# Sparse-window attention and a two-layer tail: q, k and x turned by crossbar DMA in batches 1 to 3, scores on half-height arrays, and GpSimd's ring for the early tiles and the weights

## The chip, the cores and the metric

The kernel runs on one core of one Trainium2 chip. The metric is device time in microseconds (us) of one execution. The core's engines are TensorE (PE: matmuls and their weight loads, PEld), VectorE (DVE), ScalarE (ACT), GpSimd (POOL) and SyncE (SP, which here only issues DMAs). Each works through its own instructions in order. Data moves by sixteen DMA engines, which SP's, ACT's and POOL's rings share.

## The reference

Four batches, eight heads, 768 positions, head size 64. A retrieval head attends to everything before it; the other heads only to the first 4 positions (the sink) and to a window of 64. The outcome of the eight heads is a row of 512 for each of 3,072 tokens, and passes through two matrices with h - tanh(h) between them.

```python
scores = q @ k.T / 8                       # (4, 8, 768, 768)
keep   = causal & (retrieval_head | key < 4 | (pos_q - pos_k < 64))
a      = softmax(where(keep, scores, -1e9))
x      = (a @ v).transpose(0, 2, 1, 3).reshape(3072, 512)
h      = x @ w_in                          # (512, 2048)
out    = (h - tanh(h)) @ w_out             # (2048, 512)
```

Which heads are retrieval heads comes as data (`is_retrieval`: three of the eight in this input).

## The kernel before

Work is cut into 12 tiles of 256 tokens, three to a batch: tile t belongs to batch t // 3, and g = t % 3 is its place in the sequence, so that attention grows with g. Within a tile the heads go in four pairs (hp); a unit n is one pair of one tile. Matmuls are in fp16.

For one unit, in order:

- `load` brings q, k and v in fp32 on SP's ring, in packets of 256 bytes (one row of one head). `cast_qk` and `cast_v` turn them to fp16; `t16` holds q and k, `v1` holds v with a column of ones, `vf` a copy of v that is zero for the heads that don't attend far.
- `st_T` turns q and k on PE (four 128x128 transposes into `tp`), then one copy takes q to `qT` and two copies take the two heads' k into `kz`. In `kz` the other head's 64 rows are zero, so that a score matmul contracts over all 128 rows.
- `st_S` (L854) multiplies k blocks by q into `sc`, ACT takes exp into `pt` (L869), DVE multiplies by a mask.
- `st_A` (L920) multiplies `pt` by v into `av`; DVE takes the reciprocal of the sum and scales (L940, L950, L964).
- `st_X`, or `st_X_tile` for ranked tiles, turns x on PE into `xp` and a copy takes it to `xT`.

For one tile, eight `H_unit`s follow (L1033: x by w_in into `ph`; ACT tanh, L1046; DVE h - tanh(h) into `gt`, L1053) and the O groups (L1092: `gt` by w_out into `po`; ACT copies to `ot`, L1068; SP stores it).

From tile 3 on a tile is *ranked*: `by_rank` has sorted the heads by their flags on the chip, and `cast_ranked` (L609, POOL) fetches each head's q, k and v at an offset read from a register, so that pairs 0 and 2 hold all retrieval heads and pairs 1 and 3 are *near* pairs, which need only the block of the query, the block before it and the sink. `st_S_near` (L798) computes near pairs. For them `kz` keeps, behind each 128 keys, a copy of the batch's first 64 keys (`repeat`, L754, POOL), so that 64 late keys of the block before and the sink's block lie side by side. If more than four heads were retrieval heads, the program would be run again in a general form; with this input it isn't.

The order of all engines is not written by hand. Each step is put down with an engine, an estimated duration and what it reads and writes (`op`), and `Plan.run` lays the steps out on the engines by those estimates and by priority; the instructions come out in that order. Which step is put down when is set by slots: slot t * 8 + u holds H unit u of tile t and the O groups of the tile before, and attention of later tiles is spread over the slots. PSUM is divided by tags: `sc` two buffers of two banks, `h` two, `m` and `o` one each.

Of the kernel before, what the change touches and what calls it, by code (L numbers as in the profile page):

```python
# [16 lines left out]
class Plan:  # L17
# [16 lines left out]
    def op(self, eng, ns, fn, r=(), w=(), dma=None, prio=None, port=False):  # L34
# [14 lines left out]
        for key in (*r, *w):  # L49
            if isinstance(key, tuple) and key[0] in self.bufs:  # L50
                tag, at = key[:2]
                deps.update(self.users.get((tag, at - self.bufs[tag]), ()))
                self.users.setdefault((tag, at), []).append(i)
# [5 lines left out]
    def run(self):  # L59
        n = len(self.ops)  # L60
        users = [[] for _ in range(n)]
# [8 lines left out]
        rings = {"SP": [], "POOL": []}  # L70
# [31 lines left out]
        while len(order) < n:  # L102
# [34 lines left out]
            if dma:  # L137
                packets, each = dma
                rings["POOL" if e == "POOL" else "SP"].append(
                    [i, t + ns + 300, each, packets * each / 16]  # L140
                )
            else:
                finish(i, t + ns + self.RESULT[e])
# [6 lines left out]
def kernel(  # L150
# [29 lines left out]
    assert n_sink_i <= 128 and window_i <= 128  # L180

    def pool(name, bufs=1, **kw):
        return ctx.enter_context(tc.tile_pool(name=name, bufs=bufs, **kw))

    const = pool("const")
    RAW, T16, PT, XB, GB, XTB, THB, OB = 6, 2, 3, 3, 3, 3, 3, 3
    bufs = dict(
        raw=RAW, t16q=T16, t16k=T16, pt=PT, x16=XB, x16t=2, rinv=XB, gt=GB, xT=XTB, th=THB, ot=OB,
        v1=2, vf=2, sc=2, m=1, h=2, o=1, **{f"qT{hp}": 2 for hp in range(HP)},
    )  # L190
    raw_pool = pool("raw", RAW)
    t16_pool = pool("t16", T16)
    qt_pool = pool("qt", 2)
    v_pool = pool("vp", 2)
    pt_pool = pool("pt", PT)
    x_pool = pool("x", XB)
    xn_pool = pool("xn", 2)
    sm_pool = pool("sm", XB)
    xt_pool = pool("xt", XTB)
    w_pool = pool("w")  # L200
    g_pool = pool("g", GB)
    th_pool = pool("th", THB)
    o_pool = pool("o", OB)
# [3 lines left out]
    HH = H // 2  # L207

    Engine = mybir.EngineType
# [12 lines left out]

    fast = n_sink_i <= 64 and window_i <= 64
    NGEN = H // 2

    KS = [192 if fast and hp % 2 else 128 for hp in range(HP)]
    kz = [
        [const.tile([128, 2, 2 * NG * KS[hp]], FP16, name=f"kz{s}_{hp}") for hp in range(HP)]
        for s in range(2)
    ]  # L230
# [13 lines left out]
    w_in_t = []  # L244
    w_out_t = []

    def program(first):
# [5 lines left out]
        def bank(shape, dt, tag, name):  # L253

            i = rot[tag] = rot.get(tag, -1) + 1
            box = []

            def get():
                if not box:
                    box.append(ps.tile(shape, dt, tag=tag, bufs=bufs[tag], name=name))  # L260
                return box[0]

            return get, (tag, i)

        def lazy(pl, shape, dt, tag, name):
            box = []

            def get():
                if not box:
                    box.append(pl.tile(shape, dt, tag=tag, name=name))  # L270
                return box[0]

            return get


        raws = {}

        def load(t, names="qkv", halves=(None,)):

            b, g = divmod(t, NG)  # L280
            for half in halves:
                h0, nh = (0, H) if half is None else (half * HH, HH)
                for nm in names:
                    src = {"q": q, "k": k, "v": v}[nm]
                    if (nm, t) not in raws:
                        idx = rot["raw"] = rot.get("raw", -1) + 1
                        raws[nm, t] = (
                            lazy(raw_pool, [128, NB, H, D], FP32, "raw", f"raw_{nm}{t}"), idx
                        )
                    r, idx = raws[nm, t]  # L290
                    for i in range(NB):
                        s0 = g * TT + i * 128
                        op(
                            "SP", max(420, 128 * nh * 1.1),
                            lambda r=r, i=i, src=src, s0=s0, h0=h0, nh=nh: nc.sync.dma_start(  # L295
                                out=r()[:, i, h0 : h0 + nh, :],
                                in_=src[b, h0 : h0 + nh, s0 : s0 + 128, :].rearrange("h p d -> p h d"),
                            ),
                            w=[("raw", idx, i, x) for x in (range(2) if half is None else (half,))],
                            dma=(128 * nh, 21.0),  # L300
                        )

        def load_w_in(j, w_after):
            w = lazy(w_pool, [128, HP, 512], FP16, f"win{j}", f"win{j}")
            op(
                "POOL", 900,
                lambda: nc.gpsimd.dma_start(
                    out=w()[:],
                    in_=moe_w_in[:, j * 512 : (j + 1) * 512].rearrange("(cb p) f -> p cb f", p=128),
                ),  # L310
                r=w_after, w=[("win", j)], dma=(512, 80.0),
            )
            w_in_t.append(w)

        def load_w_out(j, w_after):
            w = lazy(w_pool, [128, 4, DM], FP16, f"wout{j}", f"wout{j}")
            op(
                "POOL", 900,
                lambda: nc.gpsimd.dma_start(
                    out=w()[:],  # L320
                    in_=moe_w_out[j * 512 : (j + 1) * 512, :].rearrange("(fb p) m -> p fb m", p=128),
                ),
                r=w_after, w=[("wout", j)], dma=(512, 80.0),
            )
            w_out_t.append(w)


        def zero_kz(eng, s, hp, c0, c1, after=()):
            op(
                eng, (c1 - c0) * 1.06 * KS[hp] / 128 + 20,  # L330
                lambda: engs[eng].memset(
                    kz[s][hp][:].bitcast(FP32)[
                        :, :, c0 * KS[hp] // 256 : c1 * KS[hp] // 256
                    ], 0.0,
                ),
                r=after, w=[("kz", s, hp, g) for g in range(c0 // TT, c1 // TT)],
            )

        if first:
            op(  # L340
                "SP", 400,
                lambda: nc.sync.dma_start(
                    out=retr_i[:], in_=is_retrieval.bitcast(I32).partition_broadcast(128)
                ),
                w=["retr"], dma=(128, 20.0),
            )
        for half in range(2):
            load(0, "qk", (half,))
            load(0, "v", (half,))
        if first:  # L350

            op("POOL", 204, lambda: nc.gpsimd.memset(ones[:], 1.0), w=["ones"])
# [5 lines left out]

# [21 lines left out]

# [16 lines left out]
            if fast:  # L397
                select(mS[0:64, 3, :], ones[0:64, :], 0.0, window_i - 65, -1, 1, "mS3")
                select(mS[64:128, 3, :], ones[64:128, :], 0.0, n_sink_i - 1, 0, -1, "mS3")

            for hp in range(HP):
                zero_kz("DVE", 0, hp, 0, TT)
            for hp in range(HP):
                zero_kz("DVE", 0, hp, TT, S)

# [19 lines left out]
            for h in range(H):  # L425
                op(
                    "DVE", 260,
# [6 lines left out]

            def make_rflag0():

                nc.vector.scalar_tensor_tensor(
                    out=rflag0[:], in0=sinks[:, 0:1].to_broadcast([128, H]), scalar=0.75,
                    in1=rflag[:], op0=ALU.is_ge, op1=ALU.max,
                )  # L440

            op("DVE", 165, make_rflag0, r=["sinks", "rflag"], w=["rflag0"])


        RANK = [4 * (hp % 2) + 2 * (hp // 2) + hh for hp in range(HP) for hh in range(2)]
        regs = {}

        def ranked(t):
            return first and fast and t >= NG

        def by_rank():

            def dve(ns, fn, r, w):
                op("DVE", ns, fn, r=r, w=w)
# [76 lines left out]
            for h in range(NGEN):  # L531
                op(
                    "DVE", 260,
# [7 lines left out]
                "DVE", 200,  # L541
# [7 lines left out]
                "DVE", 150,  # L549
# [14 lines left out]
        t16s = {}  # L564

        def cast_op(e, ns, dst, src, r, w):
            cost = {"ACT": 163 + 0.85 * ns, "DVE": 85 + 0.65 * ns, "POOL": 90 + 0.96 * ns}[e]
            if e == "ACT":
                op(e, cost, lambda: nc.scalar.copy(out=dst(), in_=src()), r=r, w=w)  # L569
            else:  # L570
                op(e, cost, lambda: engs[e].tensor_copy(out=dst(), in_=src()), r=r, w=w, port=True)

        def cast_qk(t, engines, halves=range(2)):

            for half in halves:
                for nm, es in zip("qk", engines):
                    if (nm, t) not in t16s:
                        t16s[nm, t] = lazy(
                            t16_pool, [128, NB, H, D], FP16, f"t16{nm}", f"t16_{nm}{t}"
                        )  # L580
                    c = t16s[nm, t]
                    r, slot = raws[nm, t]
# [693 lines left out]
```

## Time and profile before

| | |
|---|---|
| median of 3 runs | 264.74 us (264.37 to 265.63) |
| span of the profiled execution | 262.6 us |
| its time beside the span | 2.1 us (median less span) |
| PE busy | 239.3 us, 91% |
| VectorE, ScalarE, GpSimd busy | 182.7, 145.0, 99.2 us |
| moved by DMA | 29.88 MB; 75,744 of 83,081 packets under 512 bytes |
| granted TensorE clock | 0.992 |

The span runs from the first to the last instruction; the rest of a run's time lies around it. PE's busy time counts matmuls from their issue to their modelled end, and neighbours overlap, so a busy PE need not be a PE at its peak. The page's other parts give the chain of waits that ended last, the groups of instructions by line and shape, and the DMA queues.

### The profile page before, as it was taken

The numbers are of one execution on the slowest core, as the hardware profiler recorded it, in microseconds if no ns is written. First come the engines' busy times: TensorE is split into PE (matmuls) and PEld (weight loads), VectorE is DVE, ScalarE is ACT, GpSimd is POOL, SyncE is SP. The second block draws the span as 40 slices with busy tenths as digits, with TensorE's granted clock in tenths as the row PEclk, the third lists the DMA queues.
The fourth block names the chain that finished last, engine by engine and source line by source line (L and its number), as shares of the span: only waits on it lengthen the run. The fifth ranks groups of instructions, "written<-read, shape, count | busy, mean of one in ns | idle before, by whom it ended". The sixth has DMA issues, their size and how long they took to land.

```text
span 262.6 us, 6565 instructions
## 1 busy us (share of the span) xinstructions
PE 239.3 (91%) x2420; PEld 177.8 (68%) x2420; DVE 182.7 (70%) x501; ACT 145.0 (55%) x215; POOL 99.2 (38%) x294
## 2 busy tenths in 40 slices
PE   0358998999999899999999999999999999999990
PEld 0146876776777677777777877777777777776660
DVE  7886975666799876678997766587897765654300
ACT  4368666765566465664566655645556747534320
POOL 5165502696994994239972300510700000000000
PEclk9999999999999999999999999999999999999996
DMA  6999999999999294457432811011001011101121
GB/s 138 222 206 194 208 197 201 207 209 241 227 215 226 76 236 99 122 129 185 88 92 57 178 40 42 2 40 41 11 35 40 2 40 42 40 4 41 40 89 46
DMA packets 83081, 29.88 MB, mean 114 GB/s; under 512 B 75744, under 2 KB 80096, under 8 KB 83040
## 3 DMA queue, kind: packets, MB, share of 16 engines
q1 hardware_dynamic: 78672, 25.05, 43.7%
q0 software_dynamic: 4224, 4.19, 9.5%
q8 instruction: 21, 0.34, 0.6%
q14 instruction: 20, 0.16, 0.2%
q10 hardware_dynamic: 144, 0.13, 0.2%
HBM read 27.27 MB, written 6.29 MB: 128 GB/s over the span
## 4 chain that ended last, share of the span: by engine, by line
PE 76%; DMA 8%; SPq 6%; DVE 5%; issue 1%; ACT 0%; POOL 0%; POOLq 0%; DVEq 0%
PE po L1092 30%; PE ph L1033 27%; DMA raw_k<-in_k_dram 8%; PE sc L854 7%; SPq L295 6%; PE av L920 5%; PE tp L716 3%; PE sc L798 2%; PE xp L982 2%; DVE pt L829 1%; DVE gt L1053 1%; DVE kz L704 1%; DVE x16t L950 1%; DVE qT L704 0%; ACT ot L1068 0%
## 5 line engine op out<-in xcount | busy, mean ns | idle before, releaser
L1033 PE MATMUL ph<-xT,win 128*128 128x256 f16 x768 | 101.3, 273 | 0.8 <-DVE gt L1053 0.7
L1092 PE MATMUL po<-wout,gt 128*128 128x512 f16 (+1 forms) x400 | 100.2, 371 | 0.3
L1046 ACT ACTIVATE th<-ph 128x512 f32<-128x512 f32 x96 | 57.4, 598 | 62.9 <-PE ph L1033 61.2
L1053 DVE SCALAR_TENSOR_TENSOR gt<-th,ph 128x512 f16<-128x512 f32 x96 | 65.6, 684 | 29.6 <-ACT th L1046 28.7
L1033 PEld LDWEIGHTS <-win 128*128 128x128 f16 x768 | 72.0, 98 | 16.5 <-DVE gt L1053 1.0
L869 ACT ACTIVATE pt<-sc 128x768 f16<-128x768 f32 (+1 forms) x60 | 53.3, 917 | 21.3 <-PE sc L854 20.7
L1092 PEld LDWEIGHTS <-gt 128*128 128x128 f16 x400 | 35.7, 98 | 20.2 <-issue 0.5
L609 POOL CAST t_q<-raw_q 128x128 f16 x72 | 21.2, 303 | 45.0 <-PE tp L716 44.6
L854 PE MATMUL sc<-qT,kz 128*128 128x256 f16 (+1 forms) x280 | 34.0, 255 | 4.6 <-DVE kz L704 3.3
L920 PEld LDWEIGHTS <-pt 128*128 128x128 f16 x552 | 26.4, 99 | 10.1 <-DVE pt L884 2.2
L854 PEld LDWEIGHTS <-kz 128*128 128x128 f16 x280 | 22.9, 100 | 12.1 <-DVE kz L704 5.6
L704 DVE COPY kz<-tp 64x256 f16<-64x256 f16 x96 | 27.2, 283 | 1.9 <-ACT qT L702 0.4
L920 PE MATMUL av<-v,pt 128*128 128x65 f16 x304 | 27.0, 197 | 1.2 <-DVE pt L884 1.2
L609 POOL CAST t_k<-raw_k 128x128 f16 x72 | 21.9, 313 | 0.1
L812 ACT ACTIVATE pt<-sc 128x1024 f16<-128x1024 f32 (+1 forms) x18 | 17.1, 950 | 8.6 <-PE sc L798 8.5
L950 DVE TENSOR_TENSOR x16t<-av,rinv 128x128 f32 x72 | 20.7, 288 | 1.5
L920 PE MATMUL av<-vf,pt 128*128 128x65 f16 x248 | 20.6, 193 | 1.1 <-DVE pt L829 0.7
L1068 ACT ACTIVATE ot<-po 128x512 f32<-128x512 f32 (+1 forms) x24 | 14.1, 589 | 10.0 <-PE po L1092 9.8
L609 POOL CAST v<-raw_v 128x128 f16 x72 | 18.8, 303 | 1.1 <-DMA raw_v<-in_v_dram 0.9
L716 PE MATMUL tp<-ident,t_q 128*128 128x128 f16 x96 | 14.0, 230 | 5.8 <-ACT t_q L569 5.3
L940 DVE RECIPROCAL rinv<-av 128x4 f32<-128x4 f32 x48 | 8.6, 180 | 15.1 <-PE av L920 14.6
L716 PEld LDWEIGHTS <-t_q 128*128 128x128 f16 x96 | 8.9, 103 | 9.6 <-ACT t_q L569 5.3
(76 smaller groups left out, 191.1 us busy)
## 6 DMA issues: line engine op xcount, KB each, us to landing
out_dram<-ot SPq DMA_DIRECT2D x23, 256.0 KB, 2.2
raw_q<-in_q_dram SPq DMA_DIRECT2D x20, 256.0 KB, 4.2
raw_k<-in_k_dram SPq DMA_DIRECT2D x20, 256.0 KB, 4.7
raw_v<-in_v_dram SPq DMA_DIRECT2D x20, 256.0 KB, 5.0
win<-in_moe_w_in_dram POOLq DMA_DIRECT2D x4, 512.0 KB, 10.6
wout<-in_moe_w_out_dram POOLq DMA_DIRECT2D x4, 512.0 KB, 12.9
raw_q<-in_q_dram SPq DMA_DIRECT2D x8, 128.0 KB, 3.4
raw_k<-in_k_dram SPq DMA_DIRECT2D x8, 128.0 KB, 3.5
```

What stands on the lines that cost most here:

```text
L609: nc.gpsimd.tensor_copy(out=o, in_=r()[:, :, at, :])
L704: nc.vector.tensor_copy(out=dst, in_=src)
L716: nc.tensor.transpose(out=tp()[:, x, i, :], in_=c()[:, i, 2 * hp : 2 * hp + 2, :], identity=ident16[:],)
L812: lambda: nc.scalar.activation(out=pt()[:, :, 0:wid], in_=sc()[:, :, 0:wid], func=AF.Exp, scale=inv_sqrt_d),
L854: nc.tensor.matmul(out=sc()[:, hh, o : o + nb * 128], lhsT=kk[:, hh, jb * KS[hp] : jb * KS[hp] + 128], rhs=qT[n]()[:, q0 * 128 : (q0 + nb) ...
L869: lambda: nc.scalar.activation(out=pt()[:, :, 512 * gi : 512 * gi + wid], in_=sc()[:, :, 0:wid], func=AF.Exp, scale=inv_sqrt_d,),
L920: nc.tensor.matmul(out=av()[:, i, hh, :], lhsT=pt()[:, hh, co : co + 128], rhs=vv, start=(jb == first_jb), stop=(jb == qb),)
L950: nc.vector.tensor_mul(out=x16s[t]()[:, :, at, :], in0=av()[:, :, hh : hh + 1, 0:D], in1=rinv()[:, :, hh : hh + 1].unsqueeze(3).to_broadca ...
L1033: nc.tensor.matmul(out=ph()[:, j, :], lhsT=w_in_t[fb // 4]()[:, cb, f0 : f0 + 128], rhs=xTs[t]()[:, cb, :], start=(cb == 0), stop=(cb == H ...
L1046: lambda: nc.scalar.activation(out=th()[:], in_=ph()[:], func=AF.Tanh, scale=1.0 / XS),
L1053: lambda: nc.vector.scalar_tensor_tensor(out=gts[t]()[:, u * FU : (u + 1) * FU, :], in0=th()[:], scalar=-XS, in1=ph()[:], op0=ALU.mult, op ...
L1092: nc.tensor.matmul(out=po()[:, c0:c1], lhsT=gts[t]()[:, f, ts * 128 : ts * 128 + 128], rhs=w_out_t[f // 4]()[:, f % 4, c0:c1], start=(f == ...
```

## The change

It rewrites much of the kernel around the same tiles, masks and second half.

- **Batch 0, tile 0.** q and k come in packets of 512 bytes (two neighbouring rows), on SP. ACT casts q, DVE casts k; PE turns them; DVE copies both into one buffer `QK` per batch, [128, 8, 768], in which each pair has one row block for q and one for k. `qT` and `kz`, its zeros and their memsets are gone. The flags of the heads come after the first half's turns, the ranking after tile 0's attention.
- **Tiles 1 and 2 and the weights.** All come on POOL's ring, the tiles already cast by the DMA (`load_cast`), in the order tile 1, w_in 0, tile 2, w_in 1 to 3, w_out 0 to 3. Two DVE copies per tile put q and k in order for PE's turn.
- **Tiles 3 to 11.** `load_raw` loads on SP, for tile 3 after w_out 2 has landed and for later ones after w_out 3. `gather` (POOL) takes q and k of a head in one copy, and SP then turns them by two crossbar transposes of [128, 1024] into `QK`. `st_X_tile` is one crossbar transpose on SP into `xT`, whose layout is now [128, block, pair, 128].
- **Scores.** Both heads of a pair are multiplied from their own 64 rows of `QK`, one after the other, into two PSUM banks. `st_S` takes one or two such units at a visit, generic and near ones mixed.
- **Near pairs.** The sink's 64 keys and the 64 late keys of each block lie ready in a buffer `kc`, [128, 2, 4, 128], filled by POOL.
- **Order.** The H units of tiles 0 and 1 alternate by w_in block; O groups follow H by two tiles instead of one; attention of tile t is spread over new stretches of slots (`cut`). The planner sees buffers across the whole program and gets a ring for ACT.

The diff at its core:

```diff
-            for i in range(NB):                      # load: 256-byte packets, SP
-                ...
+    def load_cast(t, after=()):
+            for x, src in enumerate((q, k)):
+                dma("POOL", 1300, lambda x=x, src=src: nc.gpsimd.dma_start(
+                        out=pk()[:].rearrange("p (x h e) -> p x h e", x=2, h=H)[:, x, :, :],
+                        in_=src[b, :, g * TT : (g + 1) * TT, :].rearrange("h (p i) d -> p h (i d)", i=2)),
+                    128 * H, 30.0, r=after, w=[("t16p", ip, x)])
+            ...
+    def load_raw(t, after=()):
+            for i in range(NB):
+                for x, src in enumerate((q, k, v)):
+                    dma("SP", 520, ..., 128 * H, 18.0, r=after, ...)
+    def gather(t):
+            for s_ in range(H):
+                def qk(s_=s_):
+                    at = bass.ds(regs["POOL"][RANK[s_]], 1)
+                    nc.gpsimd.tensor_copy(out=c5()[:, :, :, s_ : s_ + 1, :], in_=r5()[:, :, :, at, :])
+                op("POOL", 400, qk, ...)
+            for i in range(NB):
+                dma("SP", 520, lambda i=i: nc.sync.dma_start_transpose(
+                        out=QKs[b]()[:, :, g * TT + i * 128 : g * TT + i * 128 + 128],
+                        in_=c()[:, i * 2 * H * D : (i + 1) * 2 * H * D]),
+                    1024, 22.0, ...)
+            ...
-    def st_S_near(n): ...
-    def st_S(n, gi): ...
+    def st_S(units):
+            todo, reads, keys, ns = [], [], [], 160
+            ...
+            def mm():
+                for n, gi, b, g, hp, near, sc, key, pieces, wid in todo:
+                    QK = QKs[b]()
+                    for jb, q0, nb, o, comp in pieces:
+                        for hh in range(2):
+                            p_ = slice(64 * hh, 64 * hh + 64)
+                            lhsT = QK[p_, HP + hp, :][:, jb * 128 : jb * 128 + 128]
+                            if comp:
+                                lhsT = kcs[b]()[p_, hp // 2, jb - 1, :]
+                            nc.tensor.matmul(out=sc()[:, hh, o : o + nb * 128], lhsT=lhsT,
+                                rhs=QK[p_, hp, q_0 : q_0 + nb * 128], start=True, stop=True)
-    def st_X_tile(t, half): ...                       # four PE transposes and a copy, twice
+    def st_X_tile(t):
+            dma("SP", 520, lambda: nc.sync.dma_start_transpose(
+                    out=xT()[:].rearrange("p i a c -> p (i a) c"),
+                    in_=xt()[:].rearrange("p i h d -> p (i h d)")), 1024, 22.0, ...)
...
-        LAG = 1
+        slots = [(t, 2 * j + u, None) for j in range(4) for t in range(2) for u in range(2)
+        ] + [(t, u, (t - 2, 4 * u)) for t in range(2, NTT) for u in range(NFU)]
+            cut = (-10.5, -6.0, 2.25, 13.5)
+            lo, hi = base + cut[g], base + cut[g + 1]
+            if ranked(t):
+                gate = [("wout", 2 if b == 1 and g == 0 else 3)]
+                spread_over([lambda t=t, gate=gate: load_raw(t, gate)], lo - 15, lo - 14)
+                spread_over([lambda t=t: gather(t), lambda t=t: spread(t)], lo - 7, lo - 5)
+                spread_over(attention(t), lo, hi)
```

More of the change, by code (lines that the diff above doesn't have):

```diff
@@ L269, in get @@
                 if not box:
-                    box.append(pl.tile(shape, dt, tag=tag, name=name))
+                    shp, dt = shape[tag]
+                    box.append(pools[tag].tile(shp, dt, tag=tag, name=f"{tag}{i}"))
                 return box[0]
-            return get
-        raws = {}
-        def load(t, names="qkv", halves=(None,)):
-            b, g = divmod(t, NG)
[L281 to L290, printed above, removed]
-                    for i in range(NB):
[L292 to L301, printed above, removed]
@@ L328, in zero_kz @@
[L328 to L346, printed above, removed]
@@ L347, in program, with dma, ranked @@
[L347 to L350, printed above, removed]
+            return get, i
+        def dma(ring, ns, fn, packets, each, r=(), w=()):
+            op(ring, ns, fn, r=r, w=w, dma=(packets, each))
+        RANK = [4 * (hp % 2) + 2 * (hp // 2) + hh for hp in range(HP) for hh in range(2)]
+        regs = {}
+        def ranked(t):
+            return first and fast and t >= NG
+        QKs, v1s, vfs, kcs, t16s, raws = {}, {}, {}, {}, {}, {}
@@ new lines, in cast_first, with fn @@
+        def cast_first(half, engines):
+            rq, iq, rv, iv = raws[0]
+            c, ic = t16s[0]
+            n = HH * 128
+            for x in range(2):
+                e = engines[x]
+                cost = {"ACT": 163 + 0.85 * n, "DVE": 85 + 0.65 * n, "POOL": 90 + 0.96 * n}[e]
+                def fn(x=x, e=e):
+                    h0 = half * HH
+                    i_ = rq()[:].rearrange("p (x h i d) -> p x i h d", x=2, h=H, i=2)[
+                        :, x, :, h0 : h0 + HH, :
+                    ]
+                    o_ = c()[:].rearrange("p (x i h d) -> p x i h d", x=2, h=H, i=2)[
+                        :, x, :, h0 : h0 + HH, :
+                    ]
+                    copy(e, o_, i_)
+                op(
+                    e, cost, fn, r=[("rawqk", iq, x, half)], w=[("t16", ic, x, half)],
+                    port=e == "DVE",
+                )
@@ L561, in by_rank @@
                 op(e, 900, get, r=["perm"], w=["regs" + e])
[L564 to L582, printed above, removed]
-                    hs = slice(half * HH, half * HH + HH)
-                    cast_op(
-                        es[half], NB * HH * D, lambda c=c, hs=hs: c()[:, :, hs, :],
-                        lambda r=r, hs=hs: r()[:, :, hs, :],
-                        r=[("raw", slot, i, half) for i in range(NB)], w=[("t16" + nm, t, half)],
-                    )
@@ L703, in copy, with st_T @@
             else:
-                nc.vector.tensor_copy(out=dst, in_=src)
-        def st_T(n, eq="DVE", ek=("DVE", "DVE")):
+                engs[e].tensor_copy(out=dst, in_=src)
+        COPY = {"ACT": 373, "DVE": 288}
+        def st_T(n, engines=("DVE", "DVE")):
             t, hp = divmod(n, HP)
             b, g = divmod(t, NG)
-            tp, key = bank([128, 2, 8, 128], FP16, "sc", f"tp{n}")
-            keys = [(*key, x) for x in range(2)]
-            cq, ck = t16s["q", t], t16s["k", t]
+            half = hp * 2 // HP
+            tp, key = bank([128, 2, NB, 128], FP16, "h", f"tp{n}")
+            keys = [key, key]
+            c, ic = t16s[t]
@@ new lines, in program @@
+        if first:
+            dma(
+                "ACT", 400,
+                lambda: nc.scalar.dma_start(
+                    out=retr_i[:], in_=is_retrieval.bitcast(I32).partition_broadcast(128)
+                ),
+                128, 20.0, w=["retr"],
+            )
+            load_first()
+            constants()
+            iq = raws[0][1]
+            for half in range(2):
+                cast_first(half, ("ACT", "DVE"))
+                for n in (2 * half, 2 * half + 1):
+                    st_T(n, TE)
+                if half == 0:
+                    flags()
+            for half in range(2):
+                for n in (2 * half, 2 * half + 1):
+                    st_S([(n, 0)])
+                if half == 0:
+                    gate = [("rawqk", iq, 0, 0)]
+                    load_cast(1, gate)
+                    for i in range(NB):
+                        cast_v_first(i)
+                    for item in ORDER:
+                        if item == "t2":
+                            load_cast(2, gate)
+                        else:
+                            load_w(*divmod(item, 4), gate)
+        else:
+            for t in range(3):
+                load_cast(t)
+            for n in range(HP):
+                st_T(n, TE)
+                st_S([(n, 0)])
@@ L1168, in program @@
+        for n in range(HP):
             st_A(n, 0)
@@ L1170, in program @@
             st_X(n, "o", "ACT")
-        for half in range(2):
-            cast_qk(1, (("ACT", "ACT"), ("ACT", "ACT")), (half,))
-            cast_v(1, ("POOL", "POOL"), (half,))
-        if first:
-            for j in range(4):
-                load_w_in(j, [("v1", 0, 1, j // 2)])
-        load(2)
-        scale_v(0, "DVE")
-        scale_v(1)
-        if first:
-            for j in range(4):
-                load_w_out(j, [("win", 3)])
-            for hp in range(HP):
-                zero_kz("POOL", 1, hp, 0, S, [("wout", 3)])
-            if fast:
-                by_rank()
@@ new lines, in program, with spread_over @@
+        if first and fast:
+            by_rank()
+        slots = [
+            (t, 2 * j + u, None) for j in range(4) for t in range(2) for u in range(2)
+        ] + [(t, u, (t - 2, 4 * u)) for t in range(2, NTT) for u in range(NFU)]
+        slot_of = {(t, u): s for s, (t, u, _) in enumerate(slots)}
+        plan = {}
+        def spread_over(fs, lo, hi):
+            for i, f in enumerate(fs):
+                plan.setdefault(max(0, int(lo + (hi - lo) * i / max(len(fs), 1))), []).append(f)
```

983 lines of the change are left out of this document (510 added, 473 removed).

## Prediction

> **What bounds the kernel now.** I read first the busy time by engine in five stretches (columns: stretch, length, then PE, PEld, DVE, ACT and POOL busy with instruction counts, granted clock, DMA share, GB/s).
>
> ```profile
> 0.00:24.72 24.72, 11.04 (x88) 7.16 (x88) 20.64 (x73) 12.56 (x22) 12.09 (x26) 1.00 1.08 190
> 24.72:66.00 41.28, 39.31 (x454) 30.58 (x455) 27.38 (x72) 27.14 (x39) 21.25 (x49) 1.00 1.13 211
> 66.00:104.00 38.00, 36.95 (x394) 27.80 (x392) 31.70 (x86) 22.32 (x32) 30.95 (x99) 1.00 0.91 183
> 104.00:248.00 144.00, 143.75 (x1435) 107.01 (x1433) 101.82 (x269) 80.79 (x119) 34.87 (x121) 1.00 0.22 60
> ```
>
> From 104 to 248 us PE is never idle and the DMA engines nearly are: there, PE work removed is time removed. Up to 24.72 us VectorE is the busy one (20.64 of 24.72). Between, PE has small gaps, and the DMA engines are full (share above 1).
>
> How dense PE is I take from the chain of waits, since busy time counts pipelined matmuls twice; then its shares by line between 104 and 160 us, which hold one whole batch.
>
> ```profile
> 105.50 0.86 PE po L1092 x4
> 106.69 0.87 PE ph L1033 x8
> 111.82 0.45 PE sc L798 x8
> 139.83 0.77 PE sc L854 x10
> ```
>
> ```profile
> by line: PE ph L1033 37.1%; PE po L1092 36.2%; PE sc L854 8.4%; PE av L920 7.0%; PE tp L716 4.4%; PE sc L798 3.8%; PE xp L982 2.4%; ACT ot L1068 1.1%; issue 0.1%
> ```
>
> A 128-wide matmul leaves every 0.45/8 = 0.056 us, an H one (256 wide) every 0.109, an O one every 0.215. Of the batch's 56 us, scores are 12.2% = 6.8 us, the q and k turns 4.4% = 2.5, the x turns 2.4% = 1.3. Then the groups by shape for the engines' prices (busy, mean ns):
>
> ```profile
> L854 PE MATMUL sc<-qT,kz 128*128 128x256 f16 x140 | 30.7, 282 | 4.3 <-DVE kz L704 3.0 <-ACT qT L702 1.2
> L704 DVE COPY kz<-tp 64x256 f16<-64x256 f16 x96 | 27.2, 283 | 1.9 <-ACT qT L702 0.4
> L609 POOL CAST t_k<-raw_k 128x128 f16 x72 | 21.9, 313 | 0.1
> L798 PE MATMUL sc<-qT,kz 128*128 128x128 f16 x132 | 10.3, 219 | 0.0
> L982 PE MATMUL xp<-ident,x16t 128*128 128x128 f16 x72 | 7.0, 219 | 0.0
> ```
>
> And the queues (packets, MB, share of 16 engines' time):
>
> ```profile
> q1 hardware_dynamic: 78672, 25.05, 43.7%
> q0 software_dynamic: 4224, 4.19, 9.5%
> ```
>
> So a small packet of SP's ring costs 0.437 x 262.6 x 16 / 78672 = 23.3 ns of one engine, a 1,024-packet load 1.5 us of all sixteen; the eight weight loads 0.095 x 262.6 = 25 us.
>
> **PE's own work.** 144 q/k turns (tiles 3 to 11) at 0.056 go: 8.1 us in all. 72 x turns: 4.0. Scores: 280 matmuls of L854 at 0.077 and 132 of L798 at 0.056 are 21.6 + 7.4 = 29.0 us. The change gives a head 64 rows, one head the upper and one the lower half of the array, with outputs in different PSUM banks, so that a pair can run at once: 14.5 us less. The trace has no half-height matmul. Bounds: no overlap (gain 0) to full overlap (14.5). I take full overlap, since rows, weights and banks of a pair are disjoint, less an edge at each st_S visit. For the edge the nearest row is L798: 219 ns for one matmul, of which 56 is its issue, so 0.16 us of pipeline. Nothing if neighbours pass without emptying it, 0.33 if it empties on the way in and out; I take 0.16. Visits: 4, 4 and 8 in batch 0, then 2, 3 and 4 per batch: 16 + 27 = 43, 6.9 us. The Trainium skill, TensorEngine Tiling (Array Packing), Key Properties, says that changing the tiling mode drains TensorE; no run here shows it yet, and without any edge the sum would be 6.9 us lower.
>
> **Start, to the end of tiles 0 to 2's attention, H of tiles 0 and 1 and O of tile 0.** Before, tile 0's last xT copy ends at 25.1 us and all of this is done at 66. Off VectorE go the kz memsets (3.7 us), the ranking (by_rank, about 4.6, now behind tile 0), scale_v (1.4, to POOL), one k cast, and tile 1's copies that slipped in. Left for tile 0: flags 3.2, two casts 0.8, eight copies 2.3, four masks 2.5, four reciprocals and products 2.4, tile 1's two rearranging copies 0.7: 12 us from about 5.5, when the first k half can have landed (its cast began at 6.0, behind four DMAs; now it is behind two). So xT is complete near 18.5 (15 if nothing waits, 25 if nothing is gained). Then ScalarE sets the pace: tile 1's exps 4 x (1.02 + 0.81) = 7.3, tile 2's 4 x 2.85 = 11.4, 16 tanh at 0.6 = 9.6, eight xT copies 3.0, two ot 1.2: 32.5 us, plus 3 us of gaps: 54 instead of 66, a gain of 12. It needs the weights in step: POOL issues 16 transfers by about 22 us (L307 took 0.8 each; twice the descriptors for the tiles, I take 1.3), and DMA work is 25 + tile 0's 7 + tiles 1 and 2's 12 = 44 us, so the last lands near 47. The casts of tiles 1 and 2 move into POOL's DMAs, and VectorE's rearranging copy waits for them with masks queued behind it; moving POOL's issues ahead of its scale_v costs nothing while ScalarE is late, up to 4 us otherwise.
>
> **Rest.** Before: 262.6 - 66 = 196.6. Less, by PE: score halves of batches 1 to 3, (168 x 0.077 + 132 x 0.056)/2 = 10.2, minus 27 edges at 0.16 = 4.3: 5.9. The 136 q/k turns left after 66 us: 7.6. x turns: 4.0. PE's gaps from 66 to 104 us were 2.0, mostly for VectorE, which loses 4.2 us per ranked tile (4 qT and 8 kz copies at 0.28, two xT at 0.42): 2.0. Together 19.5.
>
> Added: tile 3's loads now wait for the third wout (near 44 us); six loads 9 us and landing 2: 55; POOL's gather of q and k (eight copies of 256 elements, between L609's 0.31 and twice that; 0.41 by its slope to the 0.62 of a 512-element cast): 3.3; two turns 4; scores to x 7; x turn 4: ready near 73. PE has H of tile 2 and O of tile 1 (14 us) from 54, to 68, and O of tile 2 if the written order has it there. So 0 to 9; I take 4. Behind the loads that wait on SP stand stores and tile 4's loads, harmless by then; behind a QK turn that waits for POOL's gather stand the last tile's x turn and stores, for which the layout leaves 2.5 slots (some 5 us) at the least. For a denser run with score pairs that need both sc buffers at once, and DMA hops in place of PE hops: 2.5 (0 to 8). POOL falls from 24 casts per tile (7.4 us) to 16 copies (5.7).
>
> The 27 crossbar turns (256 KB each) show in no trace. The nearest row is a load of the same size: 1.5 us of the engines, 4.2 to 5.0 from issue to landing. Below: not under 0, the bytes move. Above: open; tile by tile PE takes 50/3 = 17 us, loads 9, stores about 2, so up to (17 - 11)/3 = 2 us each hides. I take 1.5, hidden, 0 us.
>
> Sum: 54 + 196.6 - 19.5 + 4 + 2.5 = 237.6. The median of the runs shown lies 264.74 - 262.6 = 2.1 above the profiled span: 240.
>
> **Rivals.** *Pairs don't overlap* (forecast's mechanism absent): for it, nothing in the trace has two matmuls in the array at once; against, disjoint rows. +10.2 after 66 us, and up to 4.3 before it, where ScalarE covers it: 250 to 254; with overlap but edges of 0.33, 27 x 0.17 = +5: 245. *The crossbar becomes the bound*: SP's ring is one queue in which the turns stand behind loads and stores, and SP waits in order. If a turn takes T of the ring, batches 1 to 3 take 9 x (11 + 3T), against 150 us of PE there; the 25 us that separate 240 from no change are used up at T = (175/9 - 11)/3 = 2.8 us, twice the load of the same size. At T = 4, 9 x 23 = 207: 240 + 57 = 297; at 3, about 270. The Trainium skill, Advanced Engine Details and Errata, X-Bar Transpose (TRN2), expects turns as fast as plain copies, 350 to 400 GB/s, which is 0.7 us each as an estimate; its section DMA Advanced Topics lists hardware descriptor generation as the worse one at transposes. No run here shows either. *Supply at the start*: 13 MB (weights, three tiles) at the 190 GB/s of the first row are 69 us, not 47; then tile 3 comes 22 us later and PE has at most 7 us more to fill it with: +15, 255; together with a slow start (25.1) 261.
>
> **How the numbers follow.** Forecast (228 to 250): 0.56. No overlap (250 to 258): 0.13. Supply (250 to 268): 0.11. Crossbar (264 upward): 0.20. The range 228 to 266 takes the first three and the crossbar's edge: low is 240 less the 27 edges (4.3), tile 3's wait (4), the looser run (2.5) and 1 us of the start; about 0.2 stays above it. A measurement of this kernel can tell 0.5%, 1.3 us. Faster by more: 0.56 + 0.13 + 0.06 of supply = 0.75; within: 0.03; slower: 0.02 of supply + 0.20 = 0.22.
>
> **What would show it.** Right: sc matmuls start in pairs, 10 in about 0.4 us; no tp or xp on PE after tile 2; H begins near 19 us; a batch in the dense stretch takes 50 us instead of 56; turns land in 3 to 5 us with no PE wait on them. Wrong: PE idle for DMA QK or xT; SP's ring full after 60 us; 256-wide score pairs 0.2 us apart; PE idle over 10 us between 50 and 80.

## The result, and the profile after

| | before | after |
|---|---|---|
| median (4 runs each, taken together) | 265.19 us (264.37 to 265.66) | 248.84 us (247.53 to 249.34) |
| ratio | | 0.937, 95% interval 0.934 to 0.941 |
| span of the profiled execution | 262.6 us | 247.3 us |
| PE, VectorE, ScalarE, GpSimd busy | 239.3, 182.7, 145.0, 99.2 us | 221.0, 148.2, 141.8, 88.0 us |
| moved by DMA | 29.88 MB | 35.33 MB |

The kernel is 6.3% faster. Forecast were 240 us, within 228 to 266: direction and range hold, and the forecast's gain is too large by 9.7 us of span (25.0 forecast, 262.6 to 237.6; 15.3 measured).

The same four stretches of the changed kernel (length, then PE, PEld, DVE, ACT, POOL busy, granted clock, DMA share, GB/s):

```profile
0.00:24.72 24.72, 9.60 (x88) 6.19 (x88) 17.73 (x47) 9.16 (x15) 18.77 (x33) 1.00 1.25 185
24.72:66.00 41.28, 36.62 (x444) 27.02 (x445) 28.90 (x75) 30.28 (x49) 15.98 (x44) 0.96 1.21 190
66.00:104.00 38.00, 36.74 (x371) 22.62 (x369) 23.21 (x55) 23.57 (x35) 24.07 (x64) 1.00 1.19 202
104.00:248.00 144.00, 138.06 (x1306) 94.29 (x1304) 78.40 (x179) 78.80 (x121) 29.21 (x82) 0.99 0.47 106
```

VectorE is relieved everywhere but in the second stretch, PE has no more to do before 66 us than it had (36.62 busy against 39.31), and the DMA engines stay full for longer. The page's slices (6.2 us each) show for how long, some 150 us; before, about 90:

```profile
DMA  5999999999998999999999993302112113001121
```

The chain of waits in the dense part (start, us, what):

```profile
168.75 0.49 PE sc L858 x10
169.24 0.98 PE ph L1052 x8
170.22 0.86 PE po L1109 x4
...
171.52 0.55 PE sc L858 x14
```

Ten score matmuls take 0.49 us; before, ten took 0.77. The H matmuls right behind them take 0.98 instead of 0.87: the edge has two sides. From the first H matmul of tile 7 to that of tile 10, one batch, there are 51.0 us; before, 57.4.

The groups by shape (busy, mean ns | idle before), and the issues of the turns (number, us from issue to landing):

```profile
L447 POOL CAST t<-rawqk 128x256 f16 x72 | 26.8, 418 | 16.3 <-DMA rawqk<-in_k_dram 16.2
...
L858 PE MATMUL sc<-QK 64*128 64x256 f16 x140 | 18.8, 288 | 2.7 <-DVE QK L757 2.4 <-ACT pt L870 0.3
```

```profile
QK<-t SPq DMA_TRANSPOSE x18, 3.7
xT<-x16t SPq DMA_TRANSPOSE x9, 3.7
```

POOL's gather takes 0.418 us a copy (estimated 0.41). A score matmul by itself is not shorter than before (288 ns, 282 before): what fell is the distance between two. The turns land 3.7 us after issue, and the waits of PE behind 64 us come to 1.2 us in all, none of them on a DMA. The queues (packets, MB, share of 16 engines):

```profile
q1 hardware_dynamic: 92320, 28.98, 59.6%
q0 software_dynamic: 12544, 5.77, 17.6%
```

**Where the gain came.** At 66 us the kernel before had begun 130 H and 42 O matmuls, 130 x 0.109 + 42 x 0.215 = 23.2 us of work. The changed kernel reaches that at 67.6 us (172 to 176 H and 20 O), with the attention of tiles 0 to 2 done in both. The kernel before had by then also begun tile 3 (10 score matmuls and 8 turns, about 1.1 us of PE), which this count leaves out. So the changed kernel starts 1.6 us *later*, and the rest takes 247.3 - 67.6 = 179.7 instead of 196.6 us. The whole gain, 16.9, lies in the rest.

### The profile page after: what moved, and what is told of

Its sections match the earlier page's. It is cut to its first block, busy times and chain, and to the rows that moved or that the text cites. A ratio compares the mean times of both kernels' runs of the same rounds, so it can differ in the third digit from the quotient of the medians.

```text
span 247.3 us, 5847 instructions
## 1 busy us (share of the span) xinstructions
PE 221.0 (89%) x2204; PEld 150.1 (61%) x2204; DVE 148.2 (60%) x354; ACT 141.8 (57%) x216; POOL 88.0 (36%) x221
## 2 busy tenths in 40 slices
DMA packets 105187, 35.33 MB, mean 143 GB/s; under 512 B 95808, under 2 KB 102208, under 8 KB 105152
## 4 chain that ended last, share of the span: by engine, by line
PE 78%; DVE 11%; ACT 4%; DMA 2%; issue 2%; DVEq 0%; SPq 0%; ACTq 0%
PE po L1109 33%; PE ph L1052 33%; PE av L942 6%; PE sc L858 6%; DVE QK L757 2%; DMA rawqk<-in_k_dram 2%; ACT pt L870 2%; DVE m L625 1%; DVE pt L912 1%; DVE pt L907 1%; DVE mS L739 1%; ACT th L1064 1%; DVE x L989 1%; DVE gt L1071 1%; ACT ot L1084 1%
## 5 line engine op out<-in xcount | busy, mean ns | idle before, releaser
L1071 DVE SCALAR_TENSOR_TENSOR gt<-th,ph 128x512 f16<-128x512 f32 x96 | 65.2, 683 | 43.7 <-ACT th L1064 43.2
L1064 ACT ACTIVATE th<-ph 128x512 f32<-128x512 f32 x96 | 57.4, 600 | 51.4 <-PE ph L1052 48.2
L870 ACT ACTIVATE pt<-sc 128x768 f16<-128x768 f32 (+1 forms) x60 | 53.6, 919 | 19.1 <-PE sc L858 16.4
L447 POOL CAST t<-rawqk 128x256 f16 x72 | 26.8, 418 | 16.3 <-DMA rawqk<-in_k_dram 16.2
L858 PE MATMUL sc<-QK 64*128 64x128 f16 (+1 forms) x364 | 24.1, 249 | 2.7 <-DVE QK L757 2.4
L974 DVE TENSOR_TENSOR x16t<-av,rinv 128x128 f32 x72 | 20.8, 289 | 1.8
L942 PEld LDWEIGHTS <-pt 128*128 128x128 f16 x420 | 17.7, 101 | 5.4 <-issue 1.8
L858 PEld LDWEIGHTS <-QK 64*128 64x128 f16 x364 | 12.8, 97 | 12.8 <-issue 8.0
L492 POOL CAST v<-rawv 128x128 f16 x72 | 19.4, 310 | 0.0
L942 PE MATMUL av<-v,pt 128*128 128x65 f16 x220 | 18.3, 201 | 0.6 <-ACT v L755 0.6
L893 DVE TENSOR_TENSOR ptn<-ptn,mS 128x512 f16<-128x512 f16 x24 | 11.7, 530 | 9.8 <-ACT ptn L870 9.7
L870 ACT ACTIVATE ptn<-sc 128x1024 f16<-128x1024 f32 (+1 forms) x18 | 17.2, 956 | 0.6 <-PE sc L858 0.6
L942 PE MATMUL av<-vf,pt 128*128 128x65 f16 x200 | 14.0, 195 | 0.0
L912 DVE TENSOR_TENSOR pt<-pt,m4r 128x1024 f16<-128x1024 f16 x12 | 9.1, 756 | 6.3 <-ACT pt L870 6.2
L296 POOL MEMSET v<- 128x48 f16 x4 | 1.2, 312 | 25.8 <-PE av L942 25.5
```

The costliest lines, as they stand in the source:

```text
L447: nc.gpsimd.tensor_copy(out=c5()[:, :, :, s_ : s_ + 1, :], in_=r5()[:, :, :, at, :])
L492: nc.gpsimd.tensor_copy(out=v1s[b]()[:, g * NB : g * NB + NB, RANK[s_] : RANK[s_] + 1, 0:D], in_=rv()[:, :, at, :],)
L858: nc.tensor.matmul(out=sc()[:, hh, o : o + nb * 128], lhsT=lhsT, rhs=QK[p_, hp, q_0 : q_0 + nb * 128], start=True, stop=True,)
L870: lambda pt=pt, sc=sc, gi=gi, wid=wid: nc.scalar.activation(out=pt()[:, :, 512 * gi : 512 * gi + wid], in_=sc()[:, :, 0:wid], func=AF.Exp, ...
L893: nc.vector.tensor_mul(out=pv, in0=pv, in1=m[:, 384:640].unsqueeze(1).to_broadcast([128, 2, 256]),)
L942: nc.tensor.matmul(out=av()[:, i, hh, :], lhsT=pt()[:, hh, co : co + 128], rhs=vv, start=(jb == first_jb), stop=(jb == qb),)
```

## Experiments

All are variants of the changed kernel (248.84) but `b_halfrows`, a variant of the kernel before. Ratios are to the kernel before, run alongside.

**Two heads in the array at once (theory: pairs overlap, an edge at each visit; rival: no overlap).** `a_headwise` issues one head's matmuls of a piece before the other's:

```diff
-                    for jb, q0, nb, o, comp in pieces:
-                        for hh in range(2):
+                    for hh in range(2):
+                        for jb, q0, nb, o, comp in pieces:
```

> The changed kernel, but within a score visit all of one head's matmuls come before the other head's, so neighbours in the stream use the same 64 rows. Theory (the score gain is the overlap of two heads in the two halves of the array): most of it is lost; batches 1 to 3 pay up to 10.2 us again, batch 0 up to 4.3 where ScalarE covers part of it: 256 to 262 us, and a 10-matmul visit takes 0.8 us instead of 0.49. Rival (PE's order does not matter, since the array runs pairs out of order, or the gain came from elsewhere): 249 us, visits stay at 0.49.

247.51 us (247.25 to 250.67), ratio 0.932 (0.929 to 0.935). No loss; whether it is a gain against 0.937 the intervals don't tell. The chain has the same price:

```profile
170.06 0.50 PE sc L858 x10
...
172.84 0.56 PE sc L858 x14
```

In the trace matmuls still start in pairs, one of each head, mostly 6 to 14 ns apart (3 to 4 in the changed kernel), although the program lists one head's first. So the overlap is real, and that it needs neighbouring pairs, as I had it, fell: the two halves of the array run down their own matmuls, and the order said above of every engine holds here within a half only. The Trainium skill, TensorEngine Tiling (Array Packing), Key Properties, says that different tiles of the array can load weights and multiply in parallel; the trace agrees.

`a_single` visits with one unit instead of two, 27 visits more in batches 1 to 3:

```diff
-                    seq.append(lambda u=units[i : i + 2]: st_S(u))
+                    (one st_S([u]) for each unit u)
```

> The changed kernel with one score unit per visit in batches 1 to 3: 18 visits per batch instead of 9. Theory (each change between half-height and full-height matmuls costs about 0.21 us, 0.10 within the scores and 0.11 behind them): 27 more visits, +5.7 us, 254.5 us. Rival (the edge is only the 0.10 within, or is covered): +2.7 or less, 249 to 251.5 us.

254.07 us (253.03 to 255.06), ratio 0.957 (0.952 to 0.962): 5.2 us more, 5.2 / 27 = 0.19 us a visit. Its chain:

```profile
161.38 0.27 PE sc L858 x4
161.66 0.98 PE ph L1052 x8
162.64 0.27 PE sc L858 x6
162.91 0.97 PE po L1109 x4
```

Four and six matmuls take 0.27 alike, and what follows takes 0.11 longer each time (0.98 for 0.87, 0.97 for 0.86).

`b_halfrows` gives the kernel before the half rows alone, the two heads alternating, with its 78 visits:

```diff
-                            lhsT=kk[:, hh, ...], rhs=qT[n]()[:, ...],
+                            lhsT=kk[p_, hh, ...], rhs=qT[n]()[p_, ...],     # p_: the head's 64 rows
```

> The kernel before with one part of the change alone: scores contract over each head's own 64 rows, the two heads alternating; zeros, turns, loads and order are kept. Theory (overlap halves 29.0 us of scores, but the kernel before makes 78 visits of one unit each, and an edge is 0.21 us): -14.5 + 16.4, of which the dense part counts -10.2 + 11.3: 264 to 267 us, no gain. Rival (edges of 0.10 or less): 255 to 259 us. Rival (no overlap at all): over 275 us.

267.64 us (266.76 to 268.05), ratio 1.007 (1.004 to 1.011). By the prices found, 14.5 us of matmuls go and 78 x 0.2 = 15.6 us of edges come: here half rows pay only where a visit holds many matmuls.

**The turns taken off PE (theory: PE's time is the kernel's time; rival: hidden anyway).** `a_xturn_pe` turns x of tiles 3 to 11 on PE again, `a_qkturn_pe` q and k (144 turns and 72 copies on VectorE):

```diff
-                lambda: nc.sync.dma_start_transpose(out=xT()..., in_=xt()...)
+                nc.tensor.transpose(out=xp()[:, p_, i, :], in_=xt()[...], identity=ident16[:])   # 72, and copies
```

> The changed kernel with x of tiles 3 to 11 turned on PE again (eight turns per tile into PSUM, two copies by VectorE) instead of by crossbar DMA. Theory (PE bounds the stretch, crossbar turns are hidden): +72 x 0.056 = +4.0 us, 253 us. Rival (the turn's 3.7 us on SP's ring costs PE waits of its own): 249 us or less.

253.82 us (253.56 to 254.87), ratio 0.957 (0.953 to 0.961): +5.0.

> The changed kernel with q and k of tiles 3 to 11 turned on PE again (144 turns, two full-height copies by VectorE per pair into the same buffer QK) instead of by crossbar DMA. Theory (PE bounds the stretch after 56 us; crossbar turns are hidden): +144 x 0.056 = +8.1 us, 257 us. Rival (the crossbar path's latency or its share of the DMA engines costs PE something before 100 us, which this gives back): 252 to 255 us.

262.5 us (259.94 to 263.05), ratio 0.988 (0.982 to 0.995): +13.7, 5.6 more than expected. The windows of 44 to 64 us show most of it. The changed kernel, then `a_qkturn_pe` (sum of the windows; PE's busy time stands behind the length):

```profile
sum 20.00, PE 19.24 PEld 14.54 DVE 12.26 ACT 13.47 POOL 11.53; mean PE 3.85 PEld 2.91 DVE 2.45 ACT 2.69 POOL 2.31
```

```profile
sum 20.00, PE 14.80 PEld 9.72 DVE 12.02 ACT 10.76 POOL 11.51; mean PE 2.96 PEld 1.94 DVE 2.40 ACT 2.15 POOL 2.30
```

```profile
POOL v L296 <- PE av L959: 17.3, 1, 17.3
DVE QK L478 <- PE tpr L462: 4.6, 2, 4.4
```

The last two rows are waits of `a_qkturn_pe` between 44 and 56 us (us in all, times, longest). POOL's gather of tile 3 stands behind a memset that waits for batch 0's attention (to 49.8 us). The copies of tile 3's turns stand at the head of VectorE's queue from 50.4 to 54.8 us with ready work behind them, and ScalarE gets no scores for 5.0 us. PE is busy 19.24 - 14.80 = 4.4 us less. That the gather is the cause is shown for a part of it alone: PE falls behind from 44 us on, before the turns, and again from 60 to 64 us, where VectorE is full (3.90 of 4). In the changed kernel it is SP that waits for the gather, and PE waits for no DMA behind 64 us. So the crossbar buys the removed work (144 x 0.056 = 8.1) and moves a wait to an engine that can afford it. 8.1 + 4.4 = 12.5 of the 13.7. The granted clock has a share too: 0.59 from 50 to 54 us and 0.984 over this run (0.991 in the changed kernel's), some 2 us; of the four runs, the one at 0.998 took 259.94.

**The turn's price (theory: 1.5 us of the engines, hidden; rival: SP's ring near its bound).** `a_turn_twice` does each of the 27 turns a second time into a spare buffer:

```diff
+        nc.sync.dma_start_transpose(out=spare..., in_=src)      # behind each turn, nobody reads it
```

> The changed kernel with each of the 27 crossbar turns done a second time into a spare buffer that nobody reads. It prices the crossbar: a turn holds SP 1.3 us and, by the packets' time, about 2.0 us of the sixteen DMA engines. Theory (turns are hidden, the DMA engines are done by 150 us and have room): the loads end later, near 190 us, PE waits little: 249 to 254 us. Rival of the prediction (the crossbar would become the bound when a turn costs 2.8 us; here a turn and its double cost 4): 270 us or more.

272.16 us (271.61 to 273.21), ratio 1.029 (1.025 to 1.032): +23.3. Its waits of PE between 60 and 200 us (us in all, times, longest), its DMA slices (6.7 us each) and its ring:

```profile
PE ph L1064 <- DMA xT<-x16t: 12.4, 5, 4.1
PE sc L870 <- DMA QK<-t: 4.6, 3, 2.1
```

```profile
DMA  5999999999999999999999999996612300710121
...
q1 hardware_dynamic: 120832, 36.06, 72.6%
```

27 more turns are 0.726 x 269.8 - 0.596 x 247.3 = 48.5 us of sixteen engines: **1.80 us a turn**. The engines are full to some 180 us, not 150, and PE waits 17.0 us for turns. Between 60 and 200 us the granted clock was 0.95 where the changed kernel had 1.00, some 7 us; the two make up the 23.3. The headroom above the changed kernel's own turns is thus less than their price: the rival's mechanism is real, it was only not reached.

**Why the start gained nothing.** Four causes were to be told apart: VectorE (17.7 of the first 24.7 us), the ranking on it, ScalarE (full from 40 to 52 us), and the supply of weights. `a_scale_dve` scales v on VectorE instead of GpSimd; `a_rank_late` puts the ranking behind tile 1:

```diff
-    SV = "POOL"
+    SV = "DVE"
```

> The changed kernel with the four products of scale_v of tiles 0 and 1 on VectorE (0.68 us each, as before the change) instead of GpSimd. Theory (at the start VectorE is the bound and is held up whenever GpSimd's product runs beside its copies: the mS copy of 128 elements took 2.71 us instead of 0.18, a mask 1.40 instead of 0.56, each while GpSimd's product ran): 3 to 4 us of such holds go, 2.7 us of products come, some of them in VectorE's idle time: 246 to 249 us, and the mS copy takes 0.2. Rival (the start is bound by loads or by PE's hops): 249 to 252 us, since VectorE only has more to do.

248.45 us (248.07 to 249.12), ratio 0.937 (0.935 to 0.940). In the changed kernel VectorE's copy of a mask block runs beside GpSimd's product (L545):

```profile
15.70 2.71 DVE L739 COPY mS<-mS 128x128 f16<-128x128 f16 x1
16.26 2.09 POOL L545 TENSOR_TENSOR vf<-v,rflag 128x520 f16<-128x520 f16 x2
```

With the product on VectorE, the copy takes 0.16 us and tile 0's last copy to xT starts at 23.9 instead of 25.8 us; the first O matmul comes at 53.9 instead of 54.9, and the total is not measurably different. This run also answers for the clock: the 0.96 in the second row of the changed kernel's stretches is a dip to about 0.5 from 31 to 35 us, and `a_scale_dve`, with 1.00 there, takes 41.2 us from its first H to the same point of work, against 41.0.

> The changed kernel with the ranking of the heads (20 small VectorE steps, 3.6 us, now between 25 and 30 us) put behind tile 1's attention. Theory (VectorE bounds the first 35 us): H of tile 0 and the turns of tile 2 come earlier, -2 to -3.5 us: 246 to 247 us. Rival (VectorE's list is not what holds the start, or the ranking then delays tile 3's gather): 249 us or more.

249.27 us (248.04 to 251.07), ratio 0.940 (0.937 to 0.943): no change.

`a_gate` makes SP really wait for the third block of W_out before all but one of tile 3's loads; in the changed kernel that order stands in the planner alone, and SP issues them from 6.7 us on:

```diff
+            if t == NG:
+                nc.gpsimd.tensor_copy(out=rq()[:, 0:1], in_=w_out_t[2][:, 0, 0:1])   # POOL, ahead of the loads
```

> The changed kernel (248.8 us) with one small GpSimd copy out of the third block of W_out into the buffer of tile 3's q and k, so that SyncE's loads of tiles 3 and 4 really wait until that block has landed; only in the planned order did they wait before, and in the trace they were issued from 6.7 us on. Supply theory: the weights land at about 45 us instead of about 57, H and O of 40 to 64 us come earlier, total 243 to 246. Pace theory (no wait of TensorE in the trace names a weight; VectorE is full from 8 to 32 us, ScalarE from 40 to 52): no change, 248.3 to 249.3, or 249.5 to 251 if tile 3 now comes too late.

248.9 us (248.73 to 249.12), ratio 0.938 (0.933 to 0.942). From issue to landing the weight blocks took, in the changed kernel and then here (min, median, max):

```profile
DMA to landing us min/median/max: 9.4/22.3/25.4
```

```profile
DMA to landing us min/median/max: 5.5/11.4/17.8
```

The last block landed at 43.2 us (issued at 25.4) instead of 57.8 (issued at 32.4), and nothing follows. `a_halfw` goes further:

```diff
+            if j > 1:
+                return                 # load_w: blocks 2 and 3 not loaded, 0 and 1 used in their place
```

> The changed kernel with two blocks of W_in and two of W_out loaded instead of four and four; the missing ones are left out and the first ones used in their place, so 2 MB less is to be brought at the start (some 10 us at the 195 GB/s of the windows from 32 to 48 us), with every instruction of the engines as before. Supply theory: 241 to 246, all of the gain before 64 us. Pace theory: 248.3 to 249.3, the same as the changed kernel.

248.21 us (247.62 to 249.66), ratio 0.935 (0.930 to 0.939): supply is not it. Last, ScalarE's share: `a_xt_dve` moves the x copies of tiles 1 and 2 to VectorE, `a_scale_xt` does that and scales v on VectorE:

```diff
-                seq += [lambda n=n: st_X(t * HP + n, "o", "ACT") for n in range(HP)]
+                seq += [lambda n=n: st_X(t * HP + n, "o", "ACT" if t == 0 else "DVE") for n in range(HP)]
```

> The changed kernel with the copies of tiles 1 and 2's x turns out of PSUM on VectorE instead of ScalarE: 8 copies of 0.37 us = 3.0 us off ScalarE, which is busy 11.8 of the 12 us from 40 to 52 while VectorE is at 8.0. Pace theory with ScalarE as the second pace: 1.5 to 3 us faster, 246 to 247.5, with TensorE's gaps between 36 and 54 us smaller. Supply theory, or VectorE as the only pace: 248.5 to 249.5.

250.09 us (249.49 to 250.91), ratio 0.942 (0.937 to 0.947).

> The same move of the x copies together with the scaling of the values on VectorE instead of GpSimd (which alone brought tile 0's last turned x from 25.8 to 23.9 us and the total to 248.45, no change). Pace theory: what was given back behind 40 us with ScalarE full is now kept, 244.5 to 246.5. Otherwise as the move alone, within 0.5 us.

248.37 us (247.82 to 249.07), ratio 0.936 (0.931 to 0.941). Both expectations missed. The timeline of one round shows how. ScalarE of the changed kernel, one round (a head pair of tile 2 and the H units beside it):

```profile
44.01 1.73 ACT L870 ACTIVATE pt<-sc 128x1024 f16<-128x1024 f32 x2
45.62 0.60 ACT L1064 ACTIVATE th<-ph 128x512 f32<-128x512 f32 x1
46.15 1.02 ACT L870 ACTIVATE pt<-sc 128x1024 f16<-128x1024 f32 x1
47.06 0.37 ACT L755 COPY xT<-xp 128x256 f16<-128x256 f16 x1
47.32 0.62 ACT L1064 ACTIVATE th<-ph 128x512 f32<-128x512 f32 x1
47.97 1.73 ACT L870 ACTIVATE pt<-sc 128x1024 f16<-128x1024 f32 x2
```

A round is 47.97 - 44.01 = 3.96 us, without a gap. In `a_xt_dve` the round begins at 44.15 and 48.37, 4.22 us, although ScalarE lost 0.37 us of it; in `a_scale_xt` it takes 4.21. From the timeline of all engines of `a_xt_dve` between 46.4 and 49 us:

```profile
46.45 0.29 DVE L757 COPY xT<-xp 128x256 f16<-128x256 f16 x1 [0.18 <-PE xp L1023]
46.66 0.68 DVE L1071 SCALAR_TENSOR_TENSOR gt<-th,ph 128x512 f16<-128x512 f32 x1
...
47.39 0.61 PE L1052 MATMUL ph<-xT,win 128*128 128x256 f16 x4 [0.55 <-DVE gt L1071]
...
47.93 0.56 PE L858 MATMUL sc<-QK 64*128 64x256 f16 x10
48.37 1.02 ACT L870 ACTIVATE pt<-sc 128x1024 f16<-128x1024 f32 x1 [0.59 <-PE sc L858]
```

The copy on VectorE stands ahead of the `gt` that frees a `ph` buffer; PE, in order, waits 0.55 us at its next H and has the next scores behind it; ScalarE waits 0.59 us for those. So this round is a loop through PE, ScalarE and VectorE, and work taken from one engine is put into the loop at another. PE is nearly full there as well (in the changed kernel busy 11.51 of the 12 us from 40 to 52), and from its first H to 67.6 us its waits come to 3.9 us in all, so that a relief of the other two had little to win. Over seven kernels (the changed one, `a_scale_dve`, `a_rank_late`, `a_gate`, `a_halfw`, `a_xt_dve`, `a_scale_xt`), the first H begins between 25.4 and 27.4 us, the first O 27.8 to 29.6 us after it, and the span ends 191.5 to 194.3 us after the first O. No single relief tried here shortens that middle by more than 0.4 us.

What would do it (an O of tile 0 earlier as a filler, a third `ph` buffer) wasn't tried and stays open. None of the variants is measurably faster than the changed kernel; `a_headwise` is the nearest.

## Why the prediction was right, and where it was off

**Right: the large terms of the rest.** One batch of the dense part takes 51.0 us instead of 57.4, 6.4 less; 50 instead of 56 was forecast.

- Halves and edges: full overlap forecast, shown. The edge was taken at 0.16 us and is 0.19 to 0.2, so scores bring 10.2 - 27 x 0.2 = 4.8 instead of 5.9. (Without any edge the sum would have been 4.3 us lower, not 6.9: it holds the 27 edges of batches 1 to 3 alone.) The nearest row (L798's pipeline) was a fair measure. The Trainium skill's rule that a change of tiling mode drains TensorE (TensorEngine Tiling (Array Packing), Key Properties) fits the trace: 0.1 us in the visit and 0.11 in the group behind it.
- q and k turns, -7.6, x turns, -4.0: undoing them costs 13.7 (8.1 of it work; the clock and waits had the rest) and 5.0.
- Three terms did not come. VectorE's relief was to give back 2.0 us of PE's gaps from 66 to 104 us; that was misread, since the row before has 38 - 36.95 = 1.05 us of gaps there, and the row after 1.26. Tile 3's wait, taken at +4 of 0 to 9, and the looser run, +2.5 of 0 to 8, stayed near 0: PE's waits behind 64 us are 1.2 us, none of them for tile 3's loads or turns. Without the three, -4.8 - 7.6 - 4.0 = -16.4 is nearly the measured -16.9. The forecast was -13.0, so 3.9 too little gain.
- The turn: taken at 1.5 us, with the rival's 2.8 as the point where nothing would be gained. It is 1.80, and hidden as the forecast had it. The Trainium skill, Advanced Engine Details and Errata, X-Bar Transpose (TRN2), expects 350 to 400 GB/s, by estimate 0.7 us a turn; the measured 1.80 decides against it.

**The failing step: the start, 54 instead of 66.** The equal point came at 67.6 us, 13.6 late. Three parts:

- A slip in the sum: the stage named (128 H and 32 O matmuls) is 20.8 us of work, but 66 us of the kernel before stood for 23.2. That is 2.4.
- "xT is complete near 18.5": 26.13 (the last copy starts at 25.76), or 7.6 late, beyond the bound given as "25 if nothing is gained". The zeros (3.7 us) and the ranking (4.6) did leave VectorE's way. But the first k was there at 6.84 us instead of 5.5 (1.3); the eight copies into `QK` held VectorE 2.84 us where the sum had 2.3 (0.5); the mask block's copy took 2.71 and one mask 1.40, where `a_scale_dve` has 0.16 and 0.55 (together 3.4); and tile 1's copies into `QK` again stood ahead of tile 0's last x (3.0, from 20.63 to 25.07). Not all of this was on the path. `a_scale_dve` shows that the 2.71 and the 1.40 come with scale_v on GpSimd, which I had as 1.4 us saved.
- "ScalarE sets the pace: 32.5, plus 3 of gaps": ScalarE was full in the trace (11.80 of the 12 us from 40 to 52), but this is a sum of one engine's work where the round shown is a loop of three, with PE nearly full too. The remaining 3.6 us are put down to it; no run sizes that part by itself.

The supply rival asked the right question with the wrong mechanism. The gate on tile 3's loads stood in the planned order alone and held nothing on the chip, the weights came some 11 us later than forecast (57.8 for 47), and that cost nothing that `a_gate` or `a_halfw` could bring back.

Too much gain in the start (13.6) and too little in the rest (3.9) leave the 9.7. That the two errors lean against each other is luck, and the start's 12 us of gain did not come at all; what carried the forecast is the work taken off PE.

## What to carry to other kernels

Half-height matmuls pay by the visit: price the change of array mode, here about 0.2 us, against the matmuls between two changes, and merge visits first. Before crediting an engine's relief in a pipelined start, follow one round through all its engines. If the round is a loop, the work moved can come back at the next engine in it. Compare two kernels at a point of equal work, counted in matmuls, and not at a named stage.

## What the runs showed of the hardware that was not expected

- The two row halves of TensorE work through their own matmuls: listed one head after the other, the two heads' matmuls still start in pairs, mostly 6 to 14 ns apart (`a_headwise`).
- A crossbar turn of 256 KB costs 1.80 us of all sixteen DMA engines, by the difference of two runs (`a_turn_twice`), more than the 1.5 worked out for a load of the same size in the kernel before.
- A 128x128 fp16 copy on VectorE took 2.71 us beside GpSimd's products and 0.16 without them (`a_scale_dve`). One 128x768 mask took 1.40 against 0.55.
